# Emptying the last y rows' PSUM banks with one VectorE copy each, spreading their moves over two queues, storing two wide jobs singly, and putting every store on Sync in a fused attention and spectral-mixing kernel

## The chip, the cores and the metric

One core of one Trainium2 chip. The metric is the device time of an execution in microseconds (us). The kernel before took a median of 437.82 us (three runs, 437.63 to 437.91). A ratio is the mean time of one kernel's runs over the mean of the other's runs of the same rounds, so it is not quite the ratio of the medians that stand beside it; the bracket behind it is its 95% interval.

## The reference, cut to what matters

```python
# B=8 batches, 8 heads x 64 = 512 channels, S=576 rows, 64 modes
x = forgetting_attention(q, k, v, f)              # (8, 576, 512)
X = rfft(x, axis=1)[:, :64]                       # 64 modes are kept
Y = X @ (w_r + 1j * w_i)                          # one 512x512 pair for each mode
u = x + irfft(Y, n=S, axis=1)                     # "y rows" are the modes' rows
out = u + relu(u @ w_ch)                          # float32, 9.44 MB
```

The weights `w_r` and `w_i` are streamed from HBM during nearly the whole kernel. Only when the last mode's weights have arrived can the last y rows be made, and with them the whole result.

## The kernel before: the parts that matter

The last group of modes leaves TensorE as two PSUM tiles of 128 partitions, 16 for each of 8 batches: `ply` (t = 0) and `plw` (t = 1, the same rows times `w_ch`). Each batch's 16 rows have to reach that batch's slot in `yy`. Batch 0's are written there by VectorE; the other seven go to an SBUF tile `yls[0]`, from which a small DMA of 16 KB (a "move") brings them to their slots.

```python
def emit_moves(yl, r0, b, t, eng):
    p0 = H4 * b
    ins = eng.dma_start(row_slot(b, t, r0, H4), yl[p0 : p0 + H4, t, :])
    if eng is nc.gpsimd:
        tc.keep_in_program_order(ins)
...
y_rows(YTl, 0, ply[:, :], plw[:, :])
nc.vector.tensor_copy(row_slot(0, 0, H2, H4), ply[0:H4, :])   # batch 0, out of PSUM
nc.scalar.copy(yls[0][:, 0, :], ply[:, :])                     # the others, out of PSUM
emit_moves(yls[0], H2, 1, 0, nc.gpsimd)
run(terms(jobs[0], ps, 0, "y"))
nc.vector.tensor_copy(row_slot(0, 1, H2, H4), plw[0:H4, :])
nc.vector.tensor_copy(yls[0][:, 1, :], plw[:, :])
emit_moves(yls[0], H2, 1, 1, nc.gpsimd)
for b in range(2, B):
    for t in range(2):
        emit_moves(yls[0], H2, b, t, nc.gpsimd)
```

Then come 20 jobs. Jobs 0 to 3 are two row blocks of 128 of batch 0 or 1; job 4 is rows 512 to 575 of both batches (two "half-height" stores from 64 partitions); jobs 5 to 9, 10 to 14 and 15 to 19 are the same for the other pairs of batches, where a "wide" job is one row block of two batches. In each, TensorE makes u and z, ScalarE copies u out of PSUM, VectorE combines them (`scalar_tensor_tensor`), and the result is stored:

```python
n_wide = 4 * (b // 2 - 1) + sb          # 0 to 3 are jobs 5 to 8
if sb == 4:                             # half-height
    for h in range(2):
        eng = nc.scalar if job is jobs[-1] and h else nc.sync
        eng.dma_start(out[b + h, 512:576, :], o[64 * h : 64 * h + 64, 0, :])
elif not wide(job):
    nc.sync.dma_start(...)              # jobs 0 to 3
elif sb % 2 or n_wide < 2:              # wide: from n_wide 2 on, two jobs share a store
    rs = slice(sb % 2 if n_wide < 2 else 0, sb % 2 + 1)
    for j, (bj, _) in enumerate(job):
        nc.sync.dma_start(out[bj, ...][:, rs, :], pair[:, j, rs, :])
```

Two blocks stored together give packets of 4 KB, a single block packets of 2 KB.

The softmax here doesn't subtract the row's maximum and nothing guards it: scores larger than these inputs give would overflow.

## Time and profile before

| | before |
|---|---|
| weight stream (DMA engines full) | to about 400 us |
| last y addition begins | 401.4 |
| first store issued, last store's data ended | 405.23, 433.86 |
| end of the span | 435.5 |

The prediction shows the page and the stretches of the end. Three details of the timeline belong to the change (columns: start, length, engine, line, operation, tiles, how many, and the idle time before with what ended it). GpSimd's issues of the late moves:

```profile
403.75 0.51 POOL L823 DMA_DIRECT2D yy<-yl  x1 [18.54 <-ACT yl L1070]
404.68 4.77 POOL L823 DMA_DIRECT2D yy<-yl  x10 [0.43 <-DVE yl L1074]
409.61 1.44 POOL L823 DMA_DIRECT2D yy<-yl  x3 [0.15 <-issue]
```

One queue issues all fourteen, one about every half microsecond, so the last goes out at 411. The first and the last store group on Sync, and the one store on ScalarE:

```profile
405.23 5.21 SPq L1017 DMA_DIRECT2D out_dram<-uo  x5
...
428.99 1.42 SPq L1013 DMA_DIRECT2D out_dram<-uo  x1
```

```profile
427.86 0.56 ACTq L1013 DMA_DIRECT2D out_dram<-uo  x1
```

ScalarE's store of the last half block is issued a microsecond before Sync issues the other half, while Sync still has 4 KB packets in flight.

### The profile page before, as it was taken

How to read it: one execution, taken by the hardware profiler on the slowest of the kernel's cores; microseconds unless marked ns; L12 is line 12 of the kernel's file. 1: busy time of each engine (PE TensorE's matmuls, PEld its weight loads, DVE VectorE, ACT ScalarE, POOL GpSimd, SP SyncE). 2: the span in 40 equal slices, each digit the busy share in tenths (PEclk: the TensorE clock that was granted, in tenths of full speed). 3: DMA queues.
4: the chain of work that ended last, by engine and by line, in shares of the span. 5: the costliest groups of instructions: out<-in, count | busy, mean ns of one | idle time of the engine just before them, and what ended most of it. 6: DMA issues, size and time to landing. Idle time of an engine off the chain costs nothing.

```text
span 435.5 us, 12294 instructions
## 1 busy us (share of the span) xinstructions
PE 361.2 (83%) x5295; PEld 245.6 (56%) x5313; DVE 264.0 (61%) x658; ACT 224.8 (52%) x340; POOL 128.6 (30%) x202
## 2 busy tenths in 40 slices
PE   3787799999987977778768797799999978989981
PEld 2353666676665655666556565666665544644440
DVE  5797788876465655546656577524324653743892
ACT  2887488774626356364364554143443442731771
POOL 7333332333233233232333222233223223200600
PEclk9997699996557668557587779599999998989997
DMA  8999999999999999999999999999999999994698
GB/s 182 234 235 240 235 236 239 235 212 237 233 215 237 225 224 237 211 236 230 216 237 212 211 211 211 212 211 211 211 211 211 211 211 211 211 211 97 225 374 293
DMA packets 50981, 97.37 MB, mean 224 GB/s; under 512 B 3792, under 2 KB 12976, under 8 KB 50928
## 3 DMA queue, kind: packets, MB, share of 16 engines
q0 software_dynamic: 46688, 86.16, 100.9%
q1 hardware_dynamic: 4160, 10.31, 6.5%
q8 instruction: 41, 0.67, 0.6%
q10 hardware_dynamic: 80, 0.13, 0.2%
q14 instruction: 12, 0.10, 0.1%
HBM read 163.73 MB, written 9.44 MB: 398 GB/s over the span
## 4 chain that ended last, share of the span: by engine, by line
PE 39%; DMA 23%; ACT 12%; DVE 10%; issue 4%; POOL 0%; DVEq 0%; ACTq 0%
DMA wb<-in_moe_w_i_dram 22%; ACT E L576 8%; PE pav L614 8%; PE A L188 7%; PE ps L569 7%; PE tp L307 5%; PE px L657 3%; DVE QTs L322 2%; PE vp L541 2%; PE pu L828 2%; ACT KT L320 2%; PE pz L828 1%; DVE XT L671 1%; DVE os L1005 1%; DVE E L591 1%
## 5 line engine op out<-in xcount | busy, mean ns | idle before, releaser
L576 ACT ACTIVATE E<-ps 128x1024 bf16<-128x1024 f32 (+1 forms) x128 | 101.5, 851 | 24.0 <-PE ps L569 13.4
L93 POOL DMA_DIRECT2D wb<-in_moe_w_r_dram x64 | 42.5, 664 | 124.8 <-PE A L188 25.0
L188 PE MATMUL A<-XT,wb 128*128 128x16 bf16 x1984 | 69.9, 181 | 10.5 <-DMA wb<-in_moe_w_i_dram 5.7
L188 PEld LDWEIGHTS <-wb 128*128 128x128 bf16 x1984 | 63.4, 100 | 24.9 <-issue 12.1
L569 PE MATMUL ps<-QTs,KT 64*128 64x64 bf16 (+4 forms) x384 | 58.2, 322 | 19.9 <-ACT E L576 17.9
L93 POOL DMA_DIRECT2D wb<-in_moe_w_i_dram x64 | 42.3, 660 | 80.7 <-DMA wb<-in_moe_w_i_dram 36.8
L614 PE MATMUL pav<-va,E 128*128 128x65 bf16 (+1 forms) x1088 | 55.2, 209 | 3.1 <-DVE x_all L636 2.6
L614 PEld LDWEIGHTS <-E 128*128 128x128 bf16 (+1 forms) x1088 | 45.3, 114 | 18.7 <-issue 9.1
L591 DVE TENSOR_TENSOR E<-E,trimask 128x256 bf16<-128x256 bf16 (+2 forms) x128 | 37.0, 303 | 20.3 <-ACT E L576 20.0
L326 ACT COPY VT<-tp 128x640 bf16<-128x640 bf16 (+1 forms) x32 | 23.2, 761 | 34.0 <-PE tp L307 34.0
L867 ACT CAST XW<-pxw 128x512 bf16<-128x512 f32 x36 | 20.7, 586 | 35.7 <-PE pxw L860 23.5
L569 PEld LDWEIGHTS <-KT 64*128 64x128 bf16 x384 | 19.1, 98 | 33.1 <-issue 21.7
L320 ACT COPY KT<-tp 128x640 bf16<-128x640 bf16 (+1 forms) x32 | 22.0, 750 | 26.4 <-PE tp L307 26.2
L910 ACT CAST XW<-pB 128x512 bf16<-128x512 f32 x36 | 20.9, 585 | 28.1 <-PE pB L828 28.0
L860 PE MATMUL pxw<-wch,yy 128*128 128x512 bf16 x133 | 33.6, 385 | 1.2 <-issue 0.7
L909 DVE CAST x_all<-pA 128x512 bf16<-128x512 f32 x36 | 24.9, 692 | 15.2 <-PE pA L828 13.4
L322 DVE COPY QTs<-tp 128x640 bf16<-128x640 bf16 (+1 forms) x32 | 23.3, 768 | 13.9 <-PE tp L307 13.7
L636 DVE TENSOR_TENSOR x_all<-pav,rcp 128x384 bf16<-128x384 f32 x64 | 29.2, 456 | 0.9
L625 DVE RECIPROCAL rcp<-pav 128x6 f32<-128x6 f32 x64 | 12.1, 190 | 24.1 <-PE pav L614 23.4
L153 DVE TENSOR_TENSOR YTe<-A,Yacc 128x128 bf16<-128x128 f32 x16 | 5.9, 368 | 33.1 <-PE A L188 33.1
L828 PEld LDWEIGHTS <-ident_bf 64*64 64x64 bf16 (+1 forms) x348 | 15.7, 109 | 17.6 <-issue 8.8
L541 PE MATMUL vp<-ident_bf,VT 128*128 128x128 bf16 x160 | 17.1, 247 | 5.2 <-DVE QTs L322 4.6
(143 smaller groups left out, 620.0 us busy)
## 6 DMA issues: line engine op xcount, KB each, us to landing
wb<-in_moe_w_r_dram POOLq DMA_DIRECT2D x62, 512.0 KB, 17.0
wb<-in_moe_w_i_dram POOLq DMA_DIRECT2D x62, 512.0 KB, 17.6
stv<-in_v_dram POOLq DMA_DIRECT2D x10, 576.0 KB, 15.2
out_dram<-os SPq DMA_DIRECT2D x10, 512.0 KB, 4.8
stk<-in_k_dram POOLq DMA_DIRECT2D x11, 288.0 KB, 15.2
stq<-in_q_dram POOLq DMA_DIRECT2D x11, 288.0 KB, 15.2
wx<-in_v_dram POOLq DMA_DIRECT2D x5, 576.0 KB, 15.5
out_dram<-uo SPq DMA_DIRECT2D x3, 512.0 KB, 4.3
```

The lines of the kernel that those rows point to most:

```text
L93: keep(nc.gpsimd.dma_start(dst, src))
L188: ins = nc.tensor.matmul(A[:, eb, mi, :], lhsT=w_of(mi, eb * 128), rhs=x_of(m), start=(i == 0), stop=(i == len(terms) - 1),)
L320: nc.scalar.copy(rows(KTs[pr % 2][:, :, 0:S]), tv)
L322: ins = nc.vector.tensor_copy(rows(QT[pr][:, :, :]), tv)
L541: nc.tensor.transpose(vp[:, sc, :, :].rearrange("p b d -> p (b d)"), VTs[s // 2 % 2][:, h, sc * 128 : (sc + 1) * 128], ident_bf[:, :],)
L569: nc.tensor.matmul(ps[:, b, o : o + n], lhsT=KTs[pr % 2][bs, h, jb * 128 : (jb + 1) * 128], rhs=QT[pr][bs, h, jb * 128 + c0 : jb * 128 + c ...
L576: nc.scalar.activation(E[:, :, piece * 512 : piece * 512 + w], ps[:, :, 0:w], ACT.Exp, scale=scale,)
L591: nc.vector.tensor_tensor(dg, dg, tr, ALU.mult)
L614: nc.tensor.matmul(pav[64 * half : 64 * half + w, slot, :], lhsT=E[:, b, c : c + (w - 1) * st + 1 : st], rhs=va[:, jb, b, :], start=(n == ...
L636: nc.vector.tensor_tensor(xo, pi, ri, ALU.mult)
L828: return nc.tensor.matmul(p, lhsT=lhsT, rhs=rhs, start=first, stop=not first, skip_group_check=True)
L860: nc.tensor.matmul(pxw[:, :], lhsT=xT[:, eb, i * 128 : (i + 1) * 128], rhs=wch[:, eb, :], start=(eb == 0), stop=(eb == NDC - 1),)
```

## The change

Its intent: each late PSUM bank is emptied by a single VectorE copy, so it comes free sooner and needs no ScalarE; the moves start on two queues at once, with the batches that are needed first in front; the first wide blocks leave as soon as they are ready; and no store runs beside another queue's.

```diff
@@ emit_moves
-            if eng is nc.gpsimd:
+            if eng is nc.gpsimd or r0 == H2:
@@ emit_o
-                        eng = nc.scalar if job is jobs[-1] and h else nc.sync
-                        eng.dma_start(
+                        nc.sync.dma_start(
...
-                elif sb % 2 or n_wide < 2:
-                    rs = slice(sb % 2 if n_wide < 2 else 0, sb % 2 + 1)
+                elif sb % 2 or n_wide < 4:
+                    rs = slice(sb % 2 if n_wide < 4 else 0, sb % 2 + 1)
@@ late rows
-        nc.vector.tensor_copy(row_slot(0, 0, H2, H4), ply[0:H4, :])
-        nc.scalar.copy(yls[0][:, 0, :], ply[:, :])
-        emit_moves(yls[0], H2, 1, 0, nc.gpsimd)
+        def late_rows(t, src):
+            keep(nc.vector.tensor_copy(yls[0][:, t, :], src))
+            keep(nc.vector.tensor_copy(row_slot(0, t, H2, H4), yls[0][0:H4, t, :]))
+            for b in (1, 2):
+                emit_moves(yls[0], H2, b, t, nc.sync)
+            for b in (3, 4):
+                emit_moves(yls[0], H2, b, t, nc.gpsimd)
+
+        late_rows(0, ply[:, :])
         run(terms(jobs[0], ps, 0, "y"))
-        nc.vector.tensor_copy(row_slot(0, 1, H2, H4), plw[0:H4, :])
-        nc.vector.tensor_copy(yls[0][:, 1, :], plw[:, :])
-        emit_moves(yls[0], H2, 1, 1, nc.gpsimd)
-        for b in range(2, B):
+        late_rows(1, plw[:, :])
+        for b in range(5, B):
```

Below, the four parts are called *copies* (the bank emptying), *moves*, *single blocks* (`n_wide < 4`) and *last store*.

## The prediction

> **What bounds the kernel now.** I started from the page. It shows a long stage in which the DMA engines never rest (the weight stream) and a short end stage:
>
> ```profile
> span 435.5 us, 12294 instructions
> ...
> DMA  8999999999999999999999999999999999994698
> GB/s 182 234 235 240 235 236 239 235 212 237 233 215 237 225 224 237 211 236 230 216 237 212 211 211 211 212 211 211 211 211 211 211 211 211 211 211 97 225 374 293
> ```
>
> The change touches only what comes after the last weight tile, that is slices 37 to 40 (one slice is 10.9 us). There the DMA digit falls once (slice 37, digit 4) and climbs to 9 again, now at 374 GB/s: those are the stores of the 9.44 MB result. So at most some 30 us are in play, and within them two candidates: the compute that makes the result, and the stores.
>
> The chain that ended last, in order of time, names compute and one move:
>
> ```profile
> 404.68 1.43 POOL yy L823 x3
> 406.12 3.42 DMA yy<-yl
> 409.53 0.04 issue
> 409.57 0.40 PE pu L828 x2
> ...
> 426.82 0.41 DVE os L1005
> 427.23 0.60 DVEq L1138
> ```
>
> Read alone, it says that the GpSimd moves of the late y rows hold TensorE until 409.53. But this chain ends with the last compute instruction at 427.8, and the program ends at 435.5: it does not contain the stores. So I asked for stretches of the end (columns: busy time by engine, granted clock, DMA share, GB/s):
>
> ```profile
> 406.80:407.20 0.40, 0.40 (x8) 0.08 (x1) 0.40 (x1) 0.40 (x1) 0.40 (x2) 1.00 0.67 151
> 407.80:408.20 0.40, 0.40 (x9) 0.21 (x4) 0.40 (x1) 0.40 (x1) 0.40 (x2) 1.00 0.52 146
> 409.60:410.20 0.60, 0.60 (x9) 0.39 (x12) 0.48 (x1) 0.18 (x1) 0.59 (x2) 1.00 0.65 200
> 411.40:411.80 0.40, 0.40 (x12) 0.28 (x8) 0.40 (x1) 0.40 (x1) 0.00 (x0) 1.00 0.56 192
> 412.00:419.80 7.80, 6.78 (x106) 3.39 (x99) 7.38 (x8) 6.56 (x8) 0.00 (x0) 1.00 1.01 372
> 419.80:430.60 10.80, 5.97 (x84) 2.96 (x78) 7.63 (x8) 5.24 (x7) 0.00 (x0) 0.95 1.00 382
> 430.60:431.60 1.00, 0.00 (x0) 0.00 (x0) 0.00 (x0) 0.00 (x0) 0.00 (x0) 0.50 0.97 248
> ```
>
> Up to 411.8 the DMA engines have four holes (share 0.52 to 0.67), one between each two jobs' stores: there the stores wait for compute. From 412 to 433 the share is 1.00: there compute waits for nothing that matters, and the end is the start of this full stretch plus the DMA work in it. Summing the store packets in order of their ends confirms it: each store's data begins where the previous one's ended, from job 3 (issued 410.11, data from about 411.6) to the last packet at 433.86. So three things can move the end: when the full stretch opens, how much DMA time its packets take, and how well its last microsecond is used.
>
> **What the Trainium skill says.** The page "DMA: Bandwidth & Descriptors", section "Issuing engines are not separate DMA queues", says that transfers issued by Scalar, Sync and GpSimd run on the same 16 DMA engines and interleave, and that several issuers only save issue time. The trace agrees: between 430.6 and 431.6, when the one ACT store runs beside Sync's, the rate is 248 GB/s at share 0.97 against 382 in the stretch before. "VectorE: DVE Perf Modes", section "Why PSUM operands drop a tier", says that a PSUM source cannot use the two-port modes; the trace has 414 ns for 16x512 bf16 from PSUM and 416 for 128x512: the partition count costs nothing, so a small copy out of PSUM is as dear as a large one. "SBUF — State Buffer", section "Who interferes with whom", says that a Vector copy in a two-port mode and a GpSimd instruction exclude each other, the later one blocking. The new row copies are SBUF to SBUF, so this can matter; no run so far shows it at this place (the k and q copies, which run beside GpSimd issues, go from 383 to 671 ns with a median near 450, which would fit).
>
> **The change part by part.**
>
> *Emptying the late banks.* In VectorE's order of time before:
>
> ```profile
> 402.12 0.41 DVE L1069 COPY yy<-ply 16x512 bf16<-16x512 bf16 x1 [0.49 <-PE ply L809]
> 402.98 0.68 DVE L1073 CAST yy<-plw 16x512 bf16<-16x512 f32 x1 [0.45 <-PE plw L813]
> 403.70 0.69 DVE L1074 CAST yl<-plw 128x512 bf16<-128x512 f32 x1
> 404.51 1.29 DVE L1005 SCALAR_TENSOR_TENSOR uo<-pz,uo 128x512 f32<-128x512 f32 x2
> ```
>
> After: bank to yl first (692 ns), then batch 0's rows from yl. For that 16x512 bf16 SBUF copy I estimate 0.29 us from two rows of the groups view: 324 ns for 640 elements per partition, 461 for 1152, so 0.27 ns an element and 153 fixed. The bank is free at 402.98+0.69 = 403.67 instead of 404.39, 0.72 earlier. But batch 0's second row comes later: before at 402.98+0.68 = 403.66, after at 403.67+0.05+0.29 = 404.01, so +0.35. Job 0's z products need that row, and the first combine (404.51) needs the products: it goes to about 404.85 and the first store from 405.23 to about 405.57. The earlier bank helps job 1's z products, which started at 404.44 just after the bank came free; but in program order they stand behind job 0's, so I count no gain. Job 1's combine, at 406.02 before, now waits for VectorE to end job 0 (404.85+1.29 = 406.14), so about +0.15. Job 3's z bank is freed by job 1's combine (products began at 407.30, combine ended 407.25), so job 3 inherits +0.15, and its store opens the full stretch. **Opening: +0.15.** The ACT copy that goes (0.58 us at 402.57) freed an idle engine: nothing.
>
> *Moves.* Batches 1 and 2 go to Sync, idle from 401.2 to 405.2; four issues of 0.59 us from 402.6 end near 405.1, just ahead of the first store. Batches 3 and 4 lead on GpSimd, from about 402.6 instead of 403.75, and the last of ten issues ends about 407.6 instead of 411.05. Batch 3's first row landed at 409.53 and held TensorE 0.39 us; now it lands near 406. What that frees is supply for a store queue which from 412 has a backlog, so on the end it counts nothing by itself. What counts is that no move is left in the full stretch. Before, 48 packets of 1 KB fell after 411.6, at about 70 ns each: 3.4 us over 16 engines is 0.21. The 128 store packets of 2 KB beside them took 103 ns instead of 85, and the 4 KB ones 166 instead of 160: another 0.2. **Moves: -0.4.**
>
> *Stores one by one.* Jobs 7 and 8 (n_wide 2 and 3) leave 1 MB as 512 packets of 2 KB, not 256 of 4 KB: 512 x 85 ns against 256 x 160 is 2.6 us more, over 16 engines **+0.16**. In exchange 512 KB can leave when job 7 ends (about 414.7) instead of at 415.85. Data of that store began at 417.14 in a queue that was full, so nothing is gained, unless earlier relief brings the queue near empty: its slack there was only about 0.35 us (issue 415.85, data 1.3 later, where the quickest store took 0.93). It is insurance.
>
> *Last store on Sync.* ACT's 64 packets took about 160 ns each where 2 KB packets on Sync took 85: 4.8 us over 16 engines is 0.30, and some 25 of Sync's packets beside them took 218 instead of 160, 0.1 more. **End: -0.4.** The cost: the last issue comes behind a Sync issue of 1.42 us (428.99), at about 430.4. With 1.0 to 1.6 us of its own that is 432.0 at worst, still near its data's turn (about 432.8).
>
> Sum: +0.15 - 0.4 + 0.16 - 0.4 = -0.5 us, from 437.8 to **437.3**.
>
> **Rivals.**
>
> *The move wait is the bound.* If what the chain shows (1.4 of issue and 3.4 of landing on batch 3) carried to the end, its 0.4 to 0.7 us would come off besides, and the faster head would fill the holes before 412, which together are worth about 0.7 us of DMA time: some 436.2. For it: VectorE is busy 7.38 of 7.80 us after 412, so a shift of its jobs persists. Against it: share 1.00 for 21 us.
>
> *The new row copies wait for GpSimd.* Its issues of batches 3 and 4 fall at 402.6 to 403.6 and from 403.7, exactly where the row copies run. One issue is 0.48 us; if VectorE loses twice, job 0 comes 0.8 late, and the opening +0.5. Then 437.7, no gain.
>
> *Sync becomes the bound.* It now issues four moves and two more stores. Its half-row stores took 0.53 to 1.59 us each, the long ones when the queue was full. If the last issue ends after 432.8, the end is set by issue and landing: up to 438.3. Against it: in the pairs before, the second issue ended over a microsecond ahead of its data (issue end 425.43, data 426.73).
>
> **Range and chances.** The terms are each known to about 0.2 or 0.3, the rivals reach from 436.2 to 438.3, and the three runs of before lie within 0.28. I take 436.3 to 438.1. Two per cent is 8.8 us, about a third of the whole end stage, and nothing here is of that size: faster 0.01, same 0.98, slower 0.01.
>
> **What would show it.** Right: VectorE's first combine near 404.85; row copies of about 0.29 us; the wait of TensorE on a move near 409.5 gone; GpSimd done by 408; share still 1.00 from 412 on and no dip of the rate near 431; last packet near 433.4. Wrong: row copies of 0.5 us or more (the lock); the holes before 412 gone and the full stretch opening before 411 (then the head was the bound and the gain is larger); a hole before the last store (Sync), or a start of the last issue after 431.5. Work before 400 should not move; if it does by over 0.3 us, the weight stream and not this change decides.

## The result, and the profile after

| | before | after |
|---|---|---|
| median of the first comparison, 6 runs each (us) | 437.73 (437.27 to 438.17) | 436.63 (436.04 to 437.05) |
| ratio | | 0.9973 [0.9961, 0.9986] |
| span of the profiled run | 435.5 | 435.3 |
| last store's data ended | 433.86 | 433.77 |

The time fell by about 1.1 us, 0.3%. All outputs are right. The two spans differ less, because one profiled run is one draw out of a spread as wide as the gain. For the same reason the last packet, which the prediction had near 433.4, ended at 433.77 in this profile.

The late part of VectorE's timeline after, which answers to the prediction's list of copies:

```profile
402.21 0.43 DVE L1069 COPY yl<-ply 128x512 bf16<-128x512 bf16 x1 [0.49 <-PE ply L809]
402.67 0.28 DVE L1070 COPY yy<-yl 16x512 bf16<-16x512 bf16 x1
403.08 0.69 DVE L1069 CAST yl<-plw 128x512 bf16<-128x512 f32 x1
403.80 0.28 DVE L1070 COPY yy<-yl 16x512 bf16<-16x512 bf16 x1
404.85 1.29 DVE L1005 SCALAR_TENSOR_TENSOR uo<-pz,uo 128x512 f32<-128x512 f32 x2 [0.77 <-DMA yy<-yl]
```

The row copies take 0.28 us and the first combine starts at 404.85, where the prediction had them. GpSimd ends its ten issues at 403.34 + 4.80 = 408.14, just past the "done by 408" of the prediction:

```profile
403.34 4.80 POOL L823 DMA_DIRECT2D yy<-yl  x10 [18.03 <-DVE yy L1070]
```

Now the stretches in which the prediction had seen holes (columns: stretch, length, busy time of TensorE, weight load, VectorE, ScalarE, GpSimd, granted clock, share of time that the DMA engines worked, GB/s). Before:

```profile
407.20:408.20 1.00, 0.92 (x13) 0.58 (x11) 0.81 (x2) 1.00 (x2) 1.00 (x3) 1.00 0.82 279
...
409.40:410.60 1.20, 1.03 (x16) 0.71 (x19) 0.80 (x2) 0.58 (x1) 1.05 (x4) 1.00 0.75 260
410.60:411.80 1.20, 1.20 (x24) 0.69 (x20) 1.20 (x2) 0.95 (x2) 0.44 (x1) 1.00 0.85 330
```

After:

```profile
407.20:408.20 1.00, 0.93 (x14) 0.54 (x10) 0.80 (x2) 1.00 (x2) 0.94 (x2) 1.00 0.27 58
...
409.40:410.60 1.20, 0.50 (x10) 0.27 (x11) 1.20 (x2) 0.98 (x1) 0.00 (x0) 1.00 1.00 401
410.60:411.80 1.20, 1.20 (x31) 0.77 (x24) 0.65 (x2) 0.43 (x1) 0.00 (x0) 1.00 1.03 410
```

This is not what the prediction said. After the change there is one deep hole at 407.2 to 408.2 (share 0.27), and from 409.4 the engines are full, at 401 to 410 GB/s; before, the rate there was 260 to 330 and the full stretch began at 411.6. From 412 on, after:

```profile
412.00:419.80 7.80, 6.60 (x100) 3.29 (x97) 7.45 (x8) 6.44 (x8) 0.00 (x0) 1.00 0.99 358
419.80:430.60 10.80, 6.17 (x88) 3.04 (x80) 7.83 (x8) 5.44 (x7) 0.00 (x0) 1.00 1.00 369
430.60:431.60 1.00, 0.00 (x0) 0.00 (x0) 0.00 (x0) 0.00 (x0) 0.00 (x0) 0.63 1.01 406
```

The share is 1.00 as before. The rate from 412 to 419.8 is lower (358 for 372), as the 2 KB packets of the single blocks would make it. The rate at 430.6 is 406 where it was 248. Sync's issues, in the order of the two groups shown of before:

```profile
405.57 4.99 SPq L1016 DMA_DIRECT2D out_dram<-uo  x5
...
429.43 2.48 SPq L1012 DMA_DIRECT2D out_dram<-uo  x2
```

The last issue ended at 431.91, well before its data's turn at 433.22, so Sync's issuing did not become the bound.

### How the parts are measured below

The clock of one execution against another hides parts of this size. In some executions of the same program TensorE is granted a lower clock shortly before the end (column with 0.66 or 1.00). Before, after, and a later execution of the changed kernel:

```profile
385.00:390.00 5.00, 5.00 (x43) 2.36 (x40) 2.22 (x4) 1.42 (x3) 0.20 (x1) 0.66 1.13 212
```

```profile
385.00:390.00 5.00, 5.00 (x48) 2.41 (x45) 2.44 (x4) 1.45 (x3) 0.31 (x1) 0.66 1.12 212
```

```profile
385.00:390.00 5.00, 4.84 (x71) 2.87 (x70) 2.77 (x5) 2.29 (x4) 0.26 (x1) 1.00 1.12 212
```

The 0.66 is a mean: in before the trace has the clock at 0.50 for 3.4 us from 385.2, and after at 0.50 for 3.4 us from 386.5. Five of the fourteen profiles have such a dip between 385 and 390. With the dip the last y addition begins 1.41 to 1.48 us after the last weight tile has landed, without it mostly 0.44 (0.78 once). That is a microsecond of chance, as large as the gain. So in each trace I count from the start of this addition (called A), and add up the store packets in order of their ends: when the first 2.25 MB (jobs 0 to 4) were out, how long the next 4.5 MB took, and how long the last 2.25 MB.

### The profile page after: what moved, and what is told of

Its sections match the earlier page's. It is cut to its first block, busy times and chain, and to the rows that moved or that the text cites. A ratio compares the mean times of both kernels' runs of the same rounds, so it can differ in the third digit from the quotient of the medians.

```text
span 435.3 us, 12316 instructions
## 1 busy us (share of the span) xinstructions
PE 360.2 (83%) x5313; PEld 244.6 (56%) x5313; DVE 263.0 (60%) x659; ACT 224.0 (51%) x339; POOL 127.0 (29%) x198
## 4 chain that ended last, share of the span: by engine, by line
DMA 39%; PE 28%; ACT 10%; DVE 8%; issue 4%; DVEq 0%; POOL 0%; ACTq 0%
DMA wb<-in_moe_w_i_dram 36%; ACT E L576 7%; PE pav L614 5%; PE ps L569 5%; PE A L188 4%; PE tp L307 4%; DMA stv<-in_v_dram 3%; PE pu L828 2%; DVE QTs L322 2%; ACT KT L320 2%; DVE os L1005 2%; PE pz L828 2%; PE vp L541 1%; PE px L657 1%; ACT VT L326 1%
## 5 line engine op out<-in xcount | busy, mean ns | idle before, releaser
L569 PE MATMUL ps<-QTs,KT 64*128 64x64 bf16 (+4 forms) x384 | 55.9, 311 | 20.3 <-ACT E L576 18.4
L614 PE MATMUL pav<-va,E 128*128 128x65 bf16 (+1 forms) x1088 | 52.8, 204 | 3.1 <-DVE x_all L636 2.6
L614 PEld LDWEIGHTS <-E 128*128 128x128 bf16 (+1 forms) x1088 | 43.2, 110 | 18.5 <-issue 9.5
L860 PE MATMUL pxw<-wch,yy 128*128 128x512 bf16 x144 | 37.0, 397 | 0.0
L860 PEld LDWEIGHTS <-yy 128*128 128x128 bf16 x144 | 12.9, 101 | 14.7 <-DVE yy L854 4.3
```

Source lines behind the costliest of these rows:

```text
L569: nc.tensor.matmul(ps[:, b, o : o + n], lhsT=KTs[pr % 2][bs, h, jb * 128 : (jb + 1) * 128], rhs=QT[pr][bs, h, jb * 128 + c0 : jb * 128 + c ...
L614: nc.tensor.matmul(pav[64 * half : 64 * half + w, slot, :], lhsT=E[:, b, c : c + (w - 1) * st + 1 : st], rhs=va[:, jb, b, :], start=(n == ...
L860: nc.tensor.matmul(pxw[:, :], lhsT=xT[:, eb, i * 128 : (i + 1) * 128], rhs=wch[:, eb, :], start=(eb == 0), stop=(eb == NDC - 1),)
```

## The experiments

Twelve runs (of five or six executions each) in three calls; each call had its own eleven runs of the kernel before. "p" kernels are the kernel before with one part of the change; "l" kernels are the changed kernel without one part. My theory was the prediction's: the end is a full DMA queue, and the parts count by the packet time they add to or take from it. The rivals were the wait on the moves, and that all of the gain is the last store, or chance.

### p_copies: the bank emptying alone

```diff
-        nc.vector.tensor_copy(row_slot(0, 0, H2, H4), ply[0:H4, :])
-        nc.scalar.copy(yls[0][:, 0, :], ply[:, :])
-        emit_moves(yls[0], H2, 1, 0, nc.gpsimd)
+        def late_rows(t, src):
+            keep(nc.vector.tensor_copy(yls[0][:, t, :], src))
+            keep(nc.vector.tensor_copy(row_slot(0, t, H2, H4), yls[0][0:H4, t, :]))
+            emit_moves(yls[0], H2, 1, t, nc.gpsimd)
+        late_rows(0, ply[:, :])      # and late_rows(1, plw[:, :]); moves in the old order
```

> The kernel before with the bank-emptying part alone (one VectorE copy of each late bank, batch 0's rows copied on from SBUF); moves all on GpSimd in the old order, stores as before. Drain theory (the end is fixed by the DMA work after 412): no more than 0.3 us either way, more likely 0 to +0.2, because the first combine goes from 404.5 to 404.85. Head theory (the gain came from an earlier start of compute): at least 0.4 us faster.

Measured: 437.73 us, ratio 0.9998 [0.9979, 1.0016]. The first 2.25 MB were out at A + 12.96 (before 12.97). Alone it shows no gain.

### p_moves: the moves alone

The kernel before with batches 1 and 2 on Sync and 3 and 4 in front on GpSimd, and the old copies:

```diff
+        def late_moves(t):
+            for b in (1, 2):
+                emit_moves(yls[0], H2, b, t, nc.sync)
+            for b in (3, 4):
+                emit_moves(yls[0], H2, b, t, nc.gpsimd)
-        emit_moves(yls[0], H2, 1, 0, nc.gpsimd)
+        late_moves(0)                # and late_moves(1); the rest from batch 5 on
```

> The kernel before with the moves alone: batches 1 and 2 on Sync, 3 and 4 first on GpSimd. Drain theory: -0.1 to -0.4 us (only the small packets after 411.6 go). Head theory: the wait of TensorE for batch 3's row at 409.5 was the bound, so 0.6 to 1.0 us faster, and the full stretch of the DMA engines opens before 411.

Measured: 437.25 us, ratio 0.9993 [0.9975, 1.0012]. First 2.25 MB at A + 12.90: nearly nothing, though TensorE no longer waits for a move and the last move lands at A + 9.64, not 13.27. Two things blur this. TensorE now waits 0.7 us for VectorE (line L1005) at a place where it waited 0.4 us for the move. And from the last landing to the end this kernel takes 1.82 us, before 1.31, because of a pause that is told under l_blocks, so its time understates what its packets show.

### p_blocks: single blocks alone

```diff
-                elif sb % 2 or n_wide < 2:
-                    rs = slice(sb % 2 if n_wide < 2 else 0, sb % 2 + 1)
+                elif sb % 2 or n_wide < 4:
+                    rs = slice(sb % 2 if n_wide < 4 else 0, sb % 2 + 1)
```

> The kernel before with jobs 7 and 8 stored one by one, nothing else. Drain theory: 1 MB in 2 KB packets instead of 4 KB costs 0.15 to 0.35 us. Head theory: the earlier store of job 7 fills a hole, 0.2 to 0.5 us faster.

Measured: 438.13 us, ratio 1.0007 [0.9988, 1.0026]. The 4.5 MB in the middle took 13.31 us (before 12.76).

### p_laststore: the last store alone

```diff
-                        eng = nc.scalar if job is jobs[-1] and h else nc.sync
-                        eng.dma_start(
+                        nc.sync.dma_start(
```

> The kernel before with only the last ACT store on Sync. Drain theory: the mixed stretch at 430.6 to 431.6 (248 GB/s) goes and the last three stores take 2.4 us of data time instead of 2.8: 0.3 to 0.5 us faster. Head theory: 0, and a Sync-issue bound would make it slower by up to 0.5 us.

Measured: 436.27 us, ratio 0.9969 [0.9951, 0.9987]: the only part that shows in the times by itself. The stretch in which before has 248 GB/s, here:

```profile
429.90:430.90 1.00, 0.00 (x0) 0.00 (x0) 0.00 (x0) 0.00 (x0) 0.00 (x0) 0.50 1.02 410
```

Its last 2.25 MB took 6.26 us, before 6.74. That is 0.5 us, less than the 1.4 that the ratio says; the interval of the ratio reaches down to 0.6.

### l_laststore: the last store back on ScalarE

The edit is the one of p_laststore, undone in the changed kernel.

> The changed kernel with its last store back on ACT, the rest of the change kept. If the last store on Sync is what gives the gain: as the kernel before or up to 0.4 us slower (the blocks cost 0.3, copies and moves give nothing), and the last 2.25 MB of stores take about 6.8 us of data time instead of 6.2. If the parts help each other (moves and copies only together): still 0.5 us or more faster than before.

Measured: 436.54 us, ratio 1.0001 [0.9988, 1.0013], against 0.9987 of the changed kernel. The slow microsecond is back:

```profile
428.50:429.50 1.00, 0.00 (x0) 0.00 (x0) 0.00 (x0) 0.00 (x0) 0.00 (x0) 0.89 1.05 406
429.50:430.50 1.00, 0.00 (x0) 0.00 (x0) 0.00 (x0) 0.00 (x0) 0.00 (x0) 0.50 0.97 254
```

Put on and taken off, the part shows in the same place with the same sign. By the expectation, though, this kernel should still have been 0.5 us faster than before if copies and moves help each other, and it was not. Its packets can be squared with that: the first 2.25 MB were out 0.52 us earlier than in before, but the middle, with its single blocks, took 0.51 us longer.

### act_pair: is it the second queue, or the half-height store?

The kernel before, with one 512 KB store of the last wide pair on ScalarE too, so that two queues run side by side with 4 KB packets for longer:

```diff
-                        nc.sync.dma_start(
+                        eng = nc.scalar if job is jobs[-2] and j else nc.sync
+                        eng.dma_start(
```

> The kernel before with one more of the last stores on ACT: batch 7's 512 KB of job 18. If two queues at once slow each other's packets: the mixed stretch grows from 0.25 to 1.25 MB and the last 2.25 MB take 7.3 us or more instead of 6.8, 0.3 to 1.0 us slower than before. If the slow packets only come from the half-height 2 KB stores: no difference. If Sync's issue time was the limit: faster.

Measured: 436.69 us, ratio 0.9997 [0.9985, 1.0008].

```profile
430.00:431.00 1.00, 0.00 (x0) 0.00 (x0) 0.00 (x0) 0.00 (x0) 0.00 (x0) 0.87 1.02 410
431.00:432.00 1.00, 0.00 (x0) 0.00 (x0) 0.00 (x0) 0.00 (x0) 0.00 (x0) 0.50 1.15 328
```

With both queues carrying 4 KB packets, each took 160 to 162 ns and the rate stayed at 410 GB/s. Only from about 431.6, when ScalarE's half-height store began beside Sync's 4 KB packets, did they slow: its 64 packets of 2 KB took 155 ns on average, and the 25 packets of 4 KB on Sync that ended after its start took 282. So "two queues slow each other" falls as a general cause. What slows is a half-height store on a second queue; whether its 64 partitions or its 2 KB packets do it was not tested, since no run has a store of 2 KB packets from all 128 partitions on a second queue.

### l_blocks and l_blocks2: the changed kernel without single blocks

The edit is the one of p_blocks, undone in the changed kernel; run twice.

> The changed kernel with jobs 7 and 8 stored as before in 512 KB stores. If the single blocks cost DMA time: 0.3 us faster than the changed kernel, about 0.6 to 1.4 us faster than before, and 4.5 MB in the middle of the stores take some 12.9 us instead of 13.2. If they are an insurance that pays: slower than the changed kernel by 0.2 us or more, with a hole in the DMA share near 415 to 417.

> The changed kernel without the single blocks, again: the version that should beat both. From the packets 0.3 us under the changed kernel of this call; if that is lost in the noise of the clock, within 0.5 us of it either way. The 4.5 MB in the middle take 12.9 to 13.1 us instead of 13.2 to 13.4.

Measured: 436.89 us, ratio 0.9996 [0.9983, 1.0008], and 436.52 us, 0.9985 [0.9972, 0.9998]; the changed kernel 0.9987 and 0.9981. The middle 4.5 MB took 13.10 and 12.91 us, with single blocks 13.2 to 13.5. The hole that the second branch of the expectation named is there too, in front of job 8's store (issued at 414.71 in l_blocks), and not in the changed kernel. First l_blocks, then after_again:

```profile
415.00:416.00 1.00, 1.00 (x24) 0.67 (x20) 0.86 (x2) 0.31 (x2) 0.00 (x0) 1.00 0.86 330
```

```profile
415.00:416.00 1.00, 0.87 (x17) 0.58 (x20) 0.86 (x3) 0.56 (x1) 0.00 (x0) 1.00 1.04 387
```

In l_blocks2 the share of the same stretch is 0.87, in the other two profiles of the changed kernel 1.01 and 1.03. So the single blocks do fill a hole, of 0.13 to 0.14 us; by the middle stretch they cost more than that.

The data ended earlier without the single blocks, but the span from the last landing to the end was 1.82 and 1.81 us, not 1.23. Sync pauses 0.42 to 0.47 us after its 79th recorded instruction in all fourteen profiles; the changed kernel has 91 on Sync and meets the pause where it waits anyway, this one has 88 and meets it after the last landing. So the version that should have beaten both did not measurably do so, and its times (0.4 and 0.2 us over the changed kernel's, the intervals overlapping) cannot tell the cost of the hole from that of the pause; moving the pause forward was not tried.

### l_copies: the changed kernel with the old bank emptying

The edit is the copies of p_moves with the rest of the change.

> The changed kernel with the late banks emptied in the old way (two VectorE copies of 16 rows out of the bank, one ACT copy). Counted from the last y addition, the first 2.25 MB of stores were out after 13.0 us without copies and moves, after 13.0 and 12.9 with one of them, and after 12.5 to 12.8 with both. If it takes both: 12.9 to 13.1 here, and a time about 0.4 us over the changed kernel's. If the moves alone do it and the earlier profile was chance: 12.5 to 12.7.

Measured: 437.10 us, ratio 0.9989 [0.9977, 1.0001]. First 2.25 MB at A + 12.84, near p_moves and just under the first branch (12.9 to 13.1). Sync and VectorE of this kernel (A = 400.75):

```profile
402.53 2.40 SPq L823 DMA_DIRECT2D yy<-yl  x4
405.03 1.83 SPq L1016 DMA_DIRECT2D out_dram<-uo  x2
```

```profile
403.05 0.69 DVE L1079 CAST yl<-plw 128x512 bf16<-128x512 f32 x1
```

and of the changed kernel (third execution, A = 400.60):

```profile
401.77 2.40 SPq L823 DMA_DIRECT2D yy<-yl  x4
404.68 4.99 SPq L1016 DMA_DIRECT2D out_dram<-uo  x5
```

```profile
402.19 0.69 DVE L1069 CAST yl<-plw 128x512 bf16<-128x512 f32 x1
402.91 0.29 DVE L1070 COPY yy<-yl 16x512 bf16<-16x512 bf16 x1
```

With the old emptying the second bank reaches `yl` at 403.05 + 0.69 = A + 2.99, because the copy of batch 0's row stands before it; Sync's four moves then last until A + 4.18 and the first store is held to A + 4.28. With the new emptying `yl` is there at A + 2.28, and the moves end at A + 3.57, half a microsecond before the first store wants Sync, at A + 4.08. So the store is issued only 0.2 us sooner than in l_copies.

### l_moves: the changed kernel with the moves back on GpSimd

```diff
-            if eng is nc.gpsimd or r0 == H2:
+            if eng is nc.gpsimd:
-            for b in (1, 2):
-                emit_moves(yls[0], H2, b, t, nc.sync)
-            for b in (3, 4):
-                emit_moves(yls[0], H2, b, t, nc.gpsimd)
+            emit_moves(yls[0], H2, 1, t, nc.gpsimd)      # the rest from batch 2 on
```

> The changed kernel with all moves on GpSimd in the old order, copies and stores as changed. If it takes both copies and moves: 12.9 to 13.1 us to the first 2.25 MB and the wait of TensorE on batch 3's row back, 0.4 us over the changed kernel. If the copies alone do it: 12.5 to 12.7.

Measured: 436.79 us, ratio 0.9995 [0.9976, 1.0014]. First 2.25 MB at A + 13.10: without the moves the copies give nothing here either. The wait of TensorE on batch 3's row, which was expected back, did not return; it waits 0.7 us for VectorE instead.

### after_again and after3: the changed kernel again

> The changed kernel once more, for a second profile of the same program and a second set of times. If the 1.63 us Sync issue and the hole behind it at 407 to 408.3 belong to the program (a 16 KB instruction fetch at 406.19 in the first profile): they stand again about 4.7 us after the last y addition. If the dip of the granted TensorE clock at 385 to 390 is chance: the last y addition lies anywhere between 400.2 and 401.6. The time should be 0.3 to 1.2 us under before.

> The changed kernel a third time, to stand beside the others of this call. First 2.25 MB at 12.5 to 12.8 us, the last 2.25 MB in 6.1 to 6.3 us; 0.5 to 1.0 us under before. The last y addition comes 0.4 us after the last weight landing if the granted clock at 385 to 390 us is 1.0, and 1.4 us after it if it is near 0.66.

Measured: 436.21 us, ratio 0.9987 [0.9973, 1.0002], and 436.44 us, 0.9981 [0.9967, 0.9995]. With the first comparison's 0.9973 the mean is 0.9980, or -0.86 us. Sync's long second issue stood again, 4.7 us after A (1.43 and 1.28 us). In after3 the clock was 1.00 and the last y addition came 0.44 us after the last weight landing, as expected; its first 2.25 MB (12.43) and its last 2.25 MB (6.53) fell outside the expected stretches.

### The traces together

All traces, counted from A (us; one profile a row):

| kernel | first 2.25 MB out | next 4.5 MB | last 2.25 MB | last landing to end |
|---|---|---|---|---|
| before | 12.97 | 12.76 | 6.74 | 1.31 |
| p_blocks | 13.03 | 13.31 | 6.76 | 1.54 |
| p_laststore | 13.09 | 13.16 | 6.26 | 1.15 |
| act_pair | 13.15 | 13.53 | 6.75 | 1.10 |
| p_copies | 12.96 | 13.09 | 7.00 | 1.31 |
| l_moves | 13.10 | 13.40 | 6.27 | 1.42 |
| p_moves | 12.90 | 12.87 | 6.85 | 1.82 |
| l_copies | 12.84 | 13.55 | 6.89 | 1.23 |
| changed kernel, three profiles | 12.84, 12.63, 12.43 | 13.22, 13.32, 13.34 | 6.21, 6.06, 6.53 | 1.23 in each |
| l_blocks, l_blocks2 | 12.50, 12.51 | 13.10, 12.91 | 6.51, 6.36 | 1.82, 1.81 |
| l_laststore | 12.45 | 13.27 | 6.65 | 1.41 |

- *First 2.25 MB.* Copies and moves together: mean 12.56 (six profiles). Neither: 13.06 (four). Copies alone 13.03, moves alone 12.87 (two each). The pair is worth -0.50, the copies alone -0.03 and the moves alone -0.19. The six profiles of the pair run from 12.43 to 12.84, so the slowest of them equals the faster one with the moves alone: that the two parts need each other is likely by these profiles, not shown.
- *Next 4.5 MB.* With single blocks 13.34 (seven), without 13.06 (seven, from 12.76 to 13.53): +0.28. Of it 0.23 is time that the engines were busy (13.06 against 12.83).
- *Last 2.25 MB.* Last store on Sync 6.39 (eight), on ScalarE 6.79 (six): -0.40. One Sync kernel, l_copies, is at 6.89. The time that the engines were busy in this stretch separates the two sides without overlap: 6.02 to 6.15 us with the store on Sync (l_copies 6.15), 6.30 to 6.40 on ScalarE, or -0.25. The rest of the -0.40 is idle time of the engines, 0.04 to 0.74 us, which in l_copies was the largest; why it varies so is open.

The sum is -0.62; the span from last landing to end adds -0.08 (1.23 for 1.31), which makes -0.70, to be held against -0.86 in the times.

Where do the -0.50 of the pair come from? I split the time up to 2.25 MB into packets of stores, small packets (most of them moves), and the rest, in which the sixteen engines idle (means, us of all sixteen engines together):

| | until 0.5 MB was out | from there to 2.25 MB | of it small packets | of it idle |
|---|---|---|---|---|
| neither part (four profiles) | 7.05 | 6.01 | 0.65 | 0.53 |
| both parts (six profiles) | 7.51 | 5.05 | 0.12 | 0.04 |
| p_moves | 7.92 | 4.98 | 0.14 | -0.02 |
| l_copies | 7.55 | 5.28 | 0.25 | 0.19 |

(-0.02 is rounding of modelled ends.) Before, half of the move packets fell among the stores of jobs 1 to 4, and holes lay between these. With the moves early, that traffic lies in front of the first stores, where the engines idle for 5 us anyway, and the stores run without a hole from 0.5 MB on. The opening pays for part of it: the first half megabyte is 0.46 later. With the moves alone the two profiles differ: p_moves gains as much behind the opening (4.98) but opens 0.87 later, while l_copies opens as with both parts (7.55) and gains less behind it (5.28). In both the moves hold the first store back to A + 4.3. So that delay does not explain by itself why the moves alone net less; it stays open.

## Why the prediction was right or wrong, point by point

**The bound: right.** From 2.25 MB on the DMA engines are nearly full in all kernels (idle at most 0.57 us of the middle stretch and 0.74 of the last), and what the chain of waits shows (TensorE held by a move until 409.53) was removed by p_moves without a clear gain in the time (with the longer end and the new wait for VectorE that are told there).

**Opening, +0.15: this step failed, in both its time and its start.** The first combine moved by +0.25 from A (3.11 to 3.36; the prediction had +0.34), but job 3's only by +0.03, since the shift was gone by then. The prediction therefore had the wrong job open the full stretch. In the changed kernel it opens with the first half megabyte, near A + 7.5 or 409.4 in the first trace, not with job 3 at 411.6; "the full stretch opening before 411" was on its list of what would prove it wrong. The half megabyte is 0.46 later, and the holes behind it, 0.49 before, are closed: the two nearly cancel.

**Moves, -0.4: the mechanism was right, the working of the size was not.** Small packets, most of them moves, did leave the stretch of the stores, worth 0.65 - 0.12 = 0.53. But the prediction counted only those after 411.6 (0.21) and reached -0.4 with a second half: store packets of 2 KB slowed to 103 ns by the moves. That half was wrong. These packets belong to job 4's half-height stores. In the three profiles of the changed kernel, with hardly a move left beside them, the 128 packets of this job took 108 to 112 ns on average, in before 101: they are slow without the moves too.

Opening and moves together were predicted at -0.25 and measured -0.50. The prediction also charged the copies with a delay alone; that they make the moves on Sync pay is what the profiles suggest, not more.

**Single blocks, +0.16: right in sign, measured +0.28.** The insurance was real: with the relief from the copies and moves the queue did run near empty, as the prediction allowed for, and l_blocks and l_blocks2 have the hole at 415 to 416 that the single blocks fill. It is smaller than what they cost.

**Last store, -0.4: right in the sum**, -0.40 in the stretch, and with the same sign in both directions of the edit. Its working is right in part: it expected all of it as packet time and 85 ns for the moved store's packets on Sync. Busy time fell by 0.25 us only, and the 128 packets of the last two stores took 103 to 108 ns on Sync; the rest is idle time, so the agreement of the sum is partly luck. Its reason needs a correction: act_pair shows that it is not the second queue as such. So the prediction's "the trace agrees" claimed too much: the drop to 248 GB/s is a loss, and the page that it cites there says only that several issuers gain no more than issue time.

**The rivals.** *The move wait* as the bound falls as worded by the packets (p_moves has the wait gone and -0.07 us at 2.25 MB; its time alone, 0.9975 to 1.0012, would not exclude it); but its second half, holes before 412 that a faster head would fill, was nearer to the truth than my step. *The lock* falls: in the third execution of the changed kernel the second row copy ran at 402.91 for 0.29 us while GpSimd was issuing (402.44 to 407.26). *Sync as the bound* falls with 431.91 against 433.22. *All of the gain is the last store* is not excluded by the times: l_laststore, which has all but that part, is at 1.0001 to before. A fit to the 106 recorded times other than act_pair's own, with one level for each call and one term for each part, gives last store -0.71 us (plus or minus 0.34), moves -0.22 (0.32), copies +0.03 (0.33), single blocks +0.19 (0.29), at 95%. Against that rival stand the packets alone.

**The total**, 437.3 predicted: measured 436.63, 436.21 and 436.44, the difference to before -1.2, -0.6 and -0.8 by ratio where -0.5 was predicted. The first median lies 0.3 above the range's lower end of 436.3, the second 0.1 below it. Errors of opposite sign (the pair too small by 0.25, the blocks by 0.12) partly cancelled.

**What stays open.** No part but the last store shows in the times with an interval that excludes 1, so the shares of the parts rest on packets of one profile for each kernel; three profiles of the changed kernel differ by 0.41 at 2.25 MB and by 0.47 in the last 2.25 MB. Also open is why Sync's second store issue takes 1.2 to 1.6 us instead of 0.34 in seven of the fourteen traces, all with the changed moves but for l_moves. It does not belong to the program: l_blocks and l_blocks2 are one kernel, and the issue took 0.34 us in the first and 1.33 in the second. A 16 KB instruction fetch begins within 0.05 us of it in several traces, but in before such a fetch began within 0.02 us of the third store's issue, which took 0.33. The hole of 407.2 to 408.2 goes with the long issue: l_blocks, without it, has a share of 0.78 a like time after A. It costs little, for both were at 2.25 MB after 12.5 us.

## What to carry to other kernels

When the DMA engines are full to the end, a wait that leads the chain can be worth nothing by itself; ask which traffic can be pushed into the idle time in front of the full stretch. Parts of a change may need each other, so measure each both put on and taken off: here the moves gave -0.19 us alone and -0.50 with the copies, in profiles whose spreads just touch. And where the gain is the size of a clock dip or a fixed pause, count packets from an event that all traces share, and run the same kernel again before believing a part.

## What the Trainium skill lacked or had wrong

- "DMA: Bandwidth & Descriptors", section "Issuing engines are not separate DMA queues": its statement that issuers interleave without a gain of their own holds for large packets (two queues of 4 KB packets: 160 to 162 ns each, 410 GB/s), but it lacks the loss when a half-height store of 2 KB packets runs beside another queue's large packets: 248 to 254 GB/s at a share of 0.97, and 6.79 us instead of 6.39 for the last 2.25 MB. The page asks for all 128 partitions for bandwidth, but gives no time for a half-height store's own packets: with no other store queue beside them, those of jobs 4, 9 and 14 took 95 to 149 ns on average, where the 2 KB packets of jobs 5 and 6, from all partitions, took 86 to 87.
- No page found gives this: a pause of 0.42 to 0.47 us on Sync after its 79th recorded instruction, in all fourteen profiles, which with 87 or 88 instructions on Sync fell into the end (1.82 us from last landing to end, not 1.23). "Runtime: NRT & Kernel Launch", section "Instruction fetch mechanics", calls the cost of crossing a block of instructions mostly hidden; no run shows that the pause is such a crossing, and no packet of an instruction fetch falls into it in any of the fourteen.
- "SBUF — State Buffer", section "Who interferes with whom", is not contradicted: the exclusion of a two-port VectorE copy and GpSimd did not show at this place; the row copies took 0.28 to 0.29 us beside GpSimd's DMA issues.
